# A two-layer decode kernel fed by one transfer queue: a new load order and new buffer places at the layer ends, and a longer rotation at the start of layer 2

## The chip, the cores and the metric

The kernel runs on one core of one Trainium2 chip. The metric is the device time of one execution in microseconds (us). Every run named here is fast, that is, not slowed by a lower granted clock.

The names of the profile are these. PE is TensorE (matrix multiply), PEld its weight loads, DVE is VectorE, ACT is ScalarE, and SP is SyncE, which here does nothing but issue transfers (DMA). "L356" is a line of the kernel that ran. The changed kernel has more lines, so the line that issues a whole K or V is L356 in the one and L359 in the other.

## The reference, cut to what matters

```python
# B, Sq, D = 2, 1, 576;  H, Sk, Dh = 32, 16384, 128;  F = 4608;  all bf16
def _A_ref(x, k_cache, v_cache, wq, wo):                    # attention over a cache
    q = (x @ wq).reshape(B, Sq, H, Dh).transpose(0, 2, 1, 3)
    scores = einsum("bhqd,bhkd->bhqk", q, k_cache) * (Dh ** -0.5)
    o = einsum("bhqk,bhkd->bhqd", softmax(scores), v_cache)
    return o.transpose(0, 2, 1, 3).reshape(B, Sq, H * Dh) @ wo
def _B_ref(x, w1, w2, w3, w4):                              # mixer and MLP
    ...                                                     # hs: small, from w2
    x1 = x + hs
    return x1 + gelu(layernorm(x1) @ w3) @ w4               # w3: 576 x 4608, w4: 4608 x 576

x = A_x                                                     # two layers, the same weights
x = x + _A_ref(layernorm(x), A_k_cache, A_v_cache, A_wq, A_wo)
x = x + _B_ref(layernorm(x), B_w1, B_w2, B_w3, B_w4)
x = x + _A_ref(layernorm(x), A_k_cache, A_v_cache, A_wq, A_wo)
x = x + _B_ref(layernorm(x), B_w1, B_w2, B_w3, B_w4)
```

Each pair of batch and head is a *unit*: 64 units a layer, each with a K of 4 MB and a V of 4 MB. The caches are read once per layer, and little is computed per byte.

## The kernel before

K(i) and V(i) stand below for the K and V of the unit at position i (0 to 63) of its layer. Layer 2 takes the units in reverse order and keeps the last two units of layer 1, so its own loads begin with K(2).

The on-chip buffer is three *places* (thirds). Each holds a K in its front half and a V in its back half. All loads go through one list in program order, on one queue:

```python
def pump(self):                              # the load list
    while self.queue:
        keys, p, n, src, sem = self.queue[0]
        under = [t for t in self.live if t["off"] < p + n and p < t["off"] + t["n"]]
        if not all(t["done"] for t in under):
            return                           # the head waits, and so does everything behind it
        ...                                  # issue it, after the last readers of what lies under it
```

This says where a unit goes, and what follows the last unit:

```python
def place(self, l, i):
    if l == 0:
        return 2 if i == self.U - 1 else i % 2
    return (2, 0, 1, 2, 0)[i] if i < 5 else (2, 1)[i % 2]
...
def want_w34(l, p):                          # w3, then w4 in pieces of 5, 4, 2, 1
    base = p * self.place_n
    rows("w3", l, self.w3, base)
    at, a0 = base + (2 * KT - 1) * self.F // 2, 0
    for c, n in enumerate(self.W4_PIECES):
        ...
        if c == 1:
            at = base                        # later pieces of w4 go over w3
...
for l in range(2):
    wp = 2 - 2 * l                           # the place of wo
    early = 5 if l == 1 else 0
    for i in range(U):
        kv("K", l, i, split=(l == 1 and i == 2))
        if i < early:
            kv("V", l, i)
        elif i - 1 >= early:
            kv("V", l, i - 1)
        ...                                  # pieces of wo; the last one where a V of place wp begins
    kv("V", l, U - 1)
    want_w34(l, 1 if l == 0 else 0)
    if l == 0:
        want_wq(1, 1)
```

In a unit, chunks 0 to 7 of K are transposed on PE, copied by ACT and multiplied on PE; chunks 8 to 15 are a multiply and a reduce each on DVE (a *pair*). The V of the unit before is weighed at the end of the unit:

```python
for i in range(U):
    ...
    dv = list(range(NCP, NCH))               # chunks 8 to 15, for DVE
    for c in range(NCP):                     # c = 0 to 7
        self.turn(l, i, c)                   # transpose chunk c
        ...
        if c >= 1:
            for _ in range(-(-len(dv) // (NCP - c))):
                self.dots(l, i, dv.pop(0))   # two pairs at c == 1, then one each
    if i >= 1:
        self.weigh(l, i - 1, 0)
    while self.waiting:
        self.score()
    if i >= 1:
        self.weigh(l, i - 1, 1)
    if i == U - 2:
        self.project_pieces(l, [self.n_wo - 1])   # last piece of wo
    ...
self.unit_max(l, U - 1)
self.exps(l, U - 1)
for h in range(2):
    self.weigh(l, U - 1, h)
self.project_last(l)
```

## Time and profile before

| before | value |
|---|---|
| time, median of 4 runs | 2590.79 us (2590.68 to 2591.45) |
| span of the profiled run | 2588.8 us |
| transfer queue busy | 99.1% of the span |
| bytes through it | 1097.76 MB |
| rate where nothing disturbs it (525 to 925 us) | 431 GB/s |
| those bytes at that rate | 1097.76 / 0.431 = 2547 us |
| DVE busy, PE busy | 76%, 59% |

These are lines of the profile's page: busy time of the engines with their instruction counts, bandwidth in 40 equal slices of the span, the main queue (packets, MB, share), and the chain of work that ended last. The last two are DVE's reduce and multiply among the costliest groups, with busy time and the mean of one in ns.

```profile
PE 1539.4 (59%) x34519; PEld 1451.9 (56%) x34519; DVE 1977.0 (76%) x2775; ACT 1111.4 (43%) x1809; POOL 0.8 (0%) x10
...
GB/s 415 429 427 432 431 431 430 429 434 431 431 430 431 430 431 432 430 432 401 423 395 359 433 432 430 431 430 431 433 430 432 430 432 430 430 433 432 429 424 343
...
q1 hardware_dynamic: 51224, 1097.76, 99.1%
...
DMA 54%; DVE 37%; PE 8%; issue 1%; ACT 0%; SPq 0%; DVEq 0%
...
L697 DVE TENSOR_REDUCE sd<-prod 128x8 f32<-128x1024 bf16 x1024 | 1249.1, 1220 | 35.5
...
L694 DVE TENSOR_TENSOR prod<-buf,qb 128x1024 bf16<-128x1024 bf16 x1024 | 697.5, 681 | 10.8 <-DMA buf<-in_A_k_cache_dram 9.9
```

The transfers are the limit: 2547 of 2588.8 us go by if the queue never pauses. A 4 MB load lands every 9.7 us, so the two loads of a unit take 19.4 us. Eight DVE pairs take 14.85 us (1.855 us a pair in the timeline, where the multiply and the reduce overlap a little). The Trainium skill's page "DMA: Bandwidth & Descriptors", section "Specifications", gives 435 GB/s as the ceiling of the fabric; the 431 GB/s of this trace lies just under it. So nothing but the dips in the bandwidth row is to be won: slice 21 (395, from 1294 us on, the layer change), slice 22 (359, from 1359 on, the start of layer 2) and the last. Slice 19 (401) dips too, but the loads around it land 9.7 us apart, so it costs nothing.

This is the windows view of before. Columns: the stretch and its length, busy us of PE, PEld, DVE, ACT and POOL (with instruction counts), granted clock of PE, share of the DMA engines, GB/s.

```profile
525.00:925.00 400.00, 231.69 (x5180) 219.38 (x5180) 307.34 (x421) 173.21 (x280) 0.00 (x0) 0.66 1.00 431
...
1268.00:1272.00 4.00, 2.31 (x46) 1.71 (x43) 3.93 (x5) 4.00 (x9) 0.00 (x0) 1.00 1.06 459
1272.00:1276.00 4.00, 3.18 (x120) 3.18 (x121) 3.90 (x6) 0.63 (x1) 0.00 (x0) 0.63 0.95 406
...
1296.00:1300.00 4.00, 3.15 (x114) 3.06 (x111) 0.23 (x1) 0.49 (x2) 0.00 (x0) 0.50 0.69 216
...
1405.00:1420.00 15.00, 9.76 (x241) 9.26 (x239) 13.84 (x19) 8.08 (x14) 0.00 (x0) 0.73 0.33 125
...
2570.00:2575.00 5.00, 3.65 (x125) 3.63 (x126) 0.88 (x7) 0.50 (x2) 0.00 (x0) 0.50 0.16 45
```

These are the issues of SP in the timeline of before, at the start of layer 2 (start, us, line, what, how many in a row):

```profile
1367.84 16.84 SPq L356 DMA_DIRECT2D buf<-in_A_k_cache_dram  x2
1384.72 0.43 SPq L356 DMA_DIRECT2D buf<-in_A_v_cache_dram  x1
1417.37 0.33 SPq L356 DMA_DIRECT2D buf<-in_A_k_cache_dram  x1
1417.74 0.43 SPq L356 DMA_DIRECT2D buf<-in_A_v_cache_dram  x1
```

The largest hole is here. K(6) and V(5) are issued by 1384.72 and land at 1400.6 and 1410.3. K(7) goes where unit 5 still computes, is issued at 1417.37 and lands at 1431.0, 20.7 us after V(5) where 9.7 is normal: 11 us lost. At 1296 to 1300 and at 2570 to 2575 the later pieces of w4 wait for w3, over which they go.

### The profile page before, as it was taken

Reading aid. Unit: us, or ns where it says so; the run is one execution under the profiler, and the core shown is the slowest. Engines: PE = TensorE matmul, PEld = TensorE weight load, DVE = VectorE, ACT = ScalarE, POOL = GpSimd, SP = SyncE. Lnnn points to the kernel's source line nnn. Section 1 sums busy time; section 2 is a strip of 40 time slices with the busy share of each in tenths; the row PEclk is TensorE's granted clock in tenths of the full one; section 3 lists DMA queues with packets and bytes.
Section 4 is the critical chain, followed back from the end, with each engine's and each line's share of the span. In section 5 each row is a group of like instructions: output and inputs, shape, how many; then the busy total and the mean of one; then the engine's idle time right before and its main releaser. Section 6 shows DMA issues by size and latency. Waiting matters only on the chain.

```text
span 2588.8 us, 75423 instructions
## 1 busy us (share of the span) xinstructions
PE 1539.4 (59%) x34519; PEld 1451.9 (56%) x34519; DVE 1977.0 (76%) x2775; ACT 1111.4 (43%) x1809; POOL 0.8 (0%) x10
## 2 busy tenths in 40 slices
PE   5656555655565556657567655556555655555575
PEld 4555555655555555546567555555554555555565
DVE  5877787778777777877759877877777777778775
ACT  4444443444444444444335444444443444444442
POOL 0000000000000000000000000000000000000000
PEclk8666666666666666666656666666666666666665
DMA  9999999999999999999998999999999999999998
GB/s 415 429 427 432 431 431 430 429 434 431 431 430 431 430 431 432 430 432 401 423 395 359 433 432 430 431 430 431 433 430 432 430 432 430 430 433 432 429 424 343
DMA packets 51322, 1099.05 MB, mean 425 GB/s; under 512 B 4820, under 2 KB 13080, under 8 KB 16792
## 3 DMA queue, kind: packets, MB, share of 16 engines
q1 hardware_dynamic: 51224, 1097.76, 99.1%
q8 instruction: 59, 0.97, 0.1%
q14 instruction: 39, 0.32, 0.0%
HBM read 1097.74 MB, written 0.00 MB: 424 GB/s over the span
## 4 chain that ended last, share of the span: by engine, by line
DMA 54%; DVE 37%; PE 8%; issue 1%; ACT 0%; SPq 0%; DVEq 0%
DMA buf<-in_A_k_cache_dram 50%; DVE sd L697 23%; DVE prod L694 13%; PE tps L665 4%; DMA buf<-in_A_v_cache_dram 2%; PE misc L715 2%; DVE small L717 1%; DMA buf<-in_A_wq_dram 1%; PE ops L738 1%; PE misc L575 0%; DMA buf<-in_B_w_dram 0%; PE sps L539 0%; SPq L370 0%; PE misc L505 0%; DVE small L709 0%
## 5 line engine op out<-in xcount | busy, mean ns | idle before, releaser
L669 ACT ACTIVATE ktsb<-tps 128x1024 bf16<-128x1024 bf16 x1024 | 1004.7, 1028 | 859.9 <-PE tps L665 854.0
L697 DVE TENSOR_REDUCE sd<-prod 128x8 f32<-128x1024 bf16 x1024 | 1249.1, 1220 | 35.5
L665 PE MATMUL tps<-ident,buf 128*128 128x128 bf16 x8192 | 833.2, 269 | 668.5 <-DMA buf<-in_A_k_cache_dram 665.8
L665 PEld LDWEIGHTS tps<-ident,buf 128*128 128x128 bf16 x8192 | 676.3, 123 | 698.2 <-DMA buf<-in_A_k_cache_dram 687.3
L694 DVE TENSOR_TENSOR prod<-buf,qb 128x1024 bf16<-128x1024 bf16 x1024 | 697.5, 681 | 10.8 <-DMA buf<-in_A_k_cache_dram 9.9
L738 PE MATMUL ops<-p,buf 128*128 128x1 bf16 x16384 | 467.5, 165 | 194.7 <-DMA buf<-in_A_v_cache_dram 180.4
L738 PEld LDWEIGHTS ops<-p,buf 128*128 128x128 bf16 x16384 | 448.7, 102 | 205.8 <-DMA buf<-in_A_v_cache_dram 188.7
L682 PE MATMUL sps<-qcur,ktsb 128*128 128x1 bf16 x8192 | 350.5, 166 | 91.3 <-ACT ktsb L669 83.1
L717 DVE TENSOR_REDUCE small<-misc 128x1 f32<-128x128 f32 x128 | 37.3, 292 | 478.8 <-PE misc L715 478.8
L682 PEld LDWEIGHTS sps<-qcur,ktsb 128*128 128x128 bf16 x8192 | 314.6, 102 | 130.2 <-ACT ktsb L669 128.3
L653 ACT ACTIVATE qb<-misc 128x128 bf16<-128x128 f32 x128 | 35.5, 278 | 519.8 <-PE misc L650 519.8
L715 PE MATMUL misc<-identS,small 128*128 128x128 f32 x256 | 95.6, 477 | 41.0 <-DVE small L709 41.0
L715 PEld LDWEIGHTS misc<-identS,small 128*128 128x128 f32 x256 | 69.7, 332 | 44.2 <-DVE small L709 35.5
L726 ACT ACTIVATE p<-sps,small 128x64 bf16<-128x64 f32 x128 | 40.7, 318 | 19.4 <-DVE small L717 19.4
L726 ACT ACTIVATE p<-sd,small 128x64 bf16<-128x64 f32 x128 | 45.3, 354 | 0.0
L645 ACT ACTIVATE qcur<-qt 128x1 bf16<-128x1 bf16 x128 | 29.1, 227 | 19.3 <-DVE qt L582 19.3
L650 PE MATMUL misc<-ident,qcur 128*128 128x128 bf16 x128 | 34.2, 267 | 1.6 <-ACT qcur L645 1.1
L705 DVE TENSOR_REDUCE small<-sps 128x1 f32<-128x64 f32 x128 | 27.4, 214 | 0.0
L726 ACT ACTIVATION_READ_ACCUMULATOR p<-sps,small 128x1 f32 x128 | 27.1, 211 | 0.0
L707 DVE TENSOR_REDUCE small<-sd 128x1 f32<-128x64 f32 x128 | 26.6, 208 | 0.0
L726 ACT ACTIVATION_READ_ACCUMULATOR p<-sd,small 128x1 f32 x128 | 26.4, 207 | 0.0
L745 DVE COPY o<-ops 128x1 f32<-128x1 f32 x128 | 18.9, 148 | 9.3 <-PE ops L738 9.3
(74 smaller groups left out, 158.8 us busy)
## 6 DMA issues: line engine op xcount, KB each, us to landing
buf<-in_A_v_cache_dram SPq DMA_DIRECT2D x126, 4096.0 KB, 31.9
buf<-in_A_k_cache_dram SPq DMA_DIRECT2D x125, 4096.0 KB, 22.5
buf<-in_B_w_dram SPq DMA_DIRECT2D x8, 1152.0 KB, 30.1
buf<-in_A_wq_dram SPq DMA_DIRECT2D x8, 1024.0 KB, 10.3
buf<-in_A_wo_dram SPq DMA_DIRECT2D x14, 576.0 KB, 32.8
buf<-in_B_w_dram SPq DMA_DIRECT2D x2, 2160.0 KB, 36.9
buf<-in_A_k_cache_dram SPq DMA_DIRECT2D x2, 2048.0 KB, 16.1
buf<-in_B_w_dram SPq DMA_DIRECT2D x2, 1728.0 KB, 8.1
```

The lines of the kernel that those rows point to most:

```text
L645: self.act(lambda a: a.activation(out=self.qcur[:, q:q + 1], in_=self.qt[:, u:u + 1], func=ACT.Copy), r=["qt"], w=[f"qcur{q}"])
L650: self.pe(lambda pe: pe.matmul(self.misc[:, 0:128], lhsT=bcast(self.qcur[:, q:q + 1], 128), rhs=self.ident[:, :], start=True, stop=True), ...
L653: self.act(lambda a: a.activation(out=self.qb[q][:, :], in_=self.misc[:, 0:128], func=ACT.Copy), r=["P:misc"], w=[f"qb{q}"])
L665: ins = pe.transpose(self.tps[b][:, j * 128:(j + 1) * 128], kt[:, (j0 + j) * 128:(j0 + j + 1) * 128], self.ident[:, :])
L669: self.act(lambda a: a.activation(out=self.ktsb[k][:, :, :].rearrange("p a b -> p (a b)"), in_=self.tps[b][:, :], func=ACT.Copy), r=[f"P:t ...
L682: ins = pe.matmul(self.sps[sp][:, col:col + 1], lhsT=self.ktsb[k][:, j, :], rhs=self.qcur[:, sp:sp + 1], start=True, stop=True)
L694: self.dve(lambda v: v.tensor_tensor(out=self.prod[d][:, :, :], in0=k3, in1=bcast_mid(self.qb[q][:, :], self.CH), op=ALU.mult), r=[*res, f ...
L697: self.dve(lambda v: v.tensor_reduce(out=self.sd[q][:, o:o + self.CH], in_=self.prod[d][:, :, :], axis=AX.X, op=ALU.add), r=[f"prod{d}"], ...
L715: self.pe(lambda pe: pe.matmul(self.misc[:, 128:256], lhsT=bcast(self.m[:, q:q + 1], 128), rhs=self.identS[:, :], start=True, stop=True), ...
L717: self.dve(lambda v: v.tensor_reduce(out=self.bias[:, q:q + 1], in_=self.misc[:, 128:256], axis=AX.X, op=ALU.max, negate=True), r=["P:misc ...
L726: self.act(lambda a, c0=c0, c1=c1, src=src, part=part: a.activation(out=self.p[q][:, c0:c1], in_=src, func=ACT.Exp, bias=self.bias[:, q:q ...
L738: ins = pe.matmul(self.ops[q][:, 0:1], lhsT=vt[:, j * 128:(j + 1) * 128], rhs=self.p[q][:, h * self.TB + j:h * self.TB + j + 1], start=(h ...
```

## The change

Its intent is to close these holes. It does five things.

1. Layer 2's first 12 units rotate over three places instead of mostly two.
2. In units 1 to 4 of layer 2, V is weighed earlier, so that its place is free sooner.
3. The later pieces of w4 go, in layer 2, into a free place instead of over w3 (and w3 itself into place 1 instead of 0).
4. At both layer ends the last K is loaded ahead of the last three Vs, and the last K and the last V come in halves. The last piece of wo, used at the end of the last unit but one in before, is now used within the last unit. The last V goes over this piece in both layers; in before it did so in layer 1 alone, and in layer 2 it changes place.
5. The wo pieces before it are used two units sooner, and the last normalizers are computed before the last V is weighed.

```diff
     def place(self, l, i):
+        if i == self.U - 1:
+            return 2 - 2 * l
         if l == 0:
-            return 2 if i == self.U - 1 else i % 2
-        return (2, 0, 1, 2, 0)[i] if i < 5 else (2, 1)[i % 2]
+            return i % 2
+        return (2, 0, 1)[i % 3] if i < self.ROT else (2, 1)[i % 2]      # ROT = 12
...
                 if c == 1:
-                    at = base
...
+                    at = p1 * self.place_n
...
-                kv("K", l, i, split=(l == 1 and i == 2))
+                kv("K", l, i, split=(l == 1 and i == 2) or i == U - 1)
                 if i < early:
-                    kv("V", l, i)
-                elif i - 1 >= early:
+                    kv("V", l, i, split=(l == 1 and i == 2))
+                elif early <= i - 1 < U - 3:
                     kv("V", l, i - 1)
...
-            kv("V", l, U - 1)
-            want_w34(l, 1 if l == 0 else 0)
+            for i in range(U - 3, U):
+                kv("V", l, i, split=i == U - 1)
+            want_w34(l, 1, 1 if l == 0 else 2)
...
+            early = l == 1 and 1 <= i <= 4
...
-                if i >= 1 and c == 4:
+                if i >= 1 and c == (3 if early else 4):
                     self.exps(l, i - 1)
...
+                if early and c == 5:
+                    self.weigh(l, i - 1, 0)
+                    self.weigh(l, i - 1, 1)
+                if i == U - 1 and c == 5:
+                    self.weigh(l, i - 2, 0)
+                    self.weigh(l, i - 2, 1)
+                    self.project_pieces(l, [self.n_wo - 1])
...                                          # wo from unit 13 on in layer 2; normalizers() and normalize() split from project()
```

More of the change, by code (lines that the diff above doesn't have):

```diff
@@ L239 @@
     N_MID = 3
+    ROT = 12
     WO_PIECE = 4
@@ L373, in want_wq, with want_w34 @@
             rows("wq", l, self.wq, p * self.place_n + unit, last=p * self.place_n + 7 * unit // 8)
-        def want_w34(l, p):
+        def want_w34(l, p, p1):
             base = p * self.place_n
@@ L381, in want_w34 @@
                 if c == 1:
-                    at = base
-                assert at + m <= (p + 1) * self.place_n
+                    assert at <= base + self.place_n
+                    at = p1 * self.place_n
                 ap = self.w4[a0 * 128 * self.FJ:(a0 + n) * 128 * self.FJ, :].rearrange(
@@ L405, in plan @@
             early = 5 if l == 1 else 0
-            gap = max(1, (U - 16) // self.n_wo)
+            wo_at = 7 if l == 0 else self.ROT + 1
+            gap = max(1, (U - 8 - wo_at) // self.n_wo)
             for i in range(U):
-                kv("K", l, i, split=(l == 1 and i == 2))
+                kv("K", l, i, split=(l == 1 and i == 2) or i == U - 1)
                 if i < early:
-                    kv("V", l, i)
-                elif i - 1 >= early:
+                    kv("V", l, i, split=(l == 1 and i == 2))
+                elif early <= i - 1 < U - 3:
                     kv("V", l, i - 1)
-                j, r = divmod(i - 7, gap)
+                j, r = divmod(i - wo_at, gap)
                 if r == 0 and 0 <= j < self.n_wo:
@@ L743, in weigh, with normalizers @@
         self.release("V", l, u, h)
-        if h == 1:
+        if h == 1 and i < self.U - 1:
             self.dve(lambda v: v.tensor_copy(out=self.o[:, u:u + 1], in_=self.ops[q][:, 0:1]),
                      r=[f"P:ops{q}"], w=["o"])
-    def project(self, l, h0, h1, parts):
-        B, D, KT = self.B, self.D, self.KT
-        u0, u1 = h0 * B, h1 * B
+    def normalizers(self, u0, u1):
         dps = self.misc[:, 320:320 + 2 * (u1 - u0)]
@@ L760, in project, with normalize @@
         self.dve(lambda v: v.reciprocal(out=den, in_=den), r=["den"], w=["den"])
-        self.dve(lambda v: v.tensor_tensor(out=self.otn[:, u0:u1], in0=self.o[:, u0:u1], in1=den, op=ALU.mult),
-                 r=["den", "o"], w=["otn"])
+    def normalize(self, u0, u1, o, res):
+        self.dve(lambda v: v.tensor_tensor(out=self.otn[:, u0:u1], in0=o, in1=self.den[:, u0:u1], op=ALU.mult),
+                 r=["den", res], w=["otn"])
+    def project(self, h0, h1, parts):
+        B, D, KT = self.B, self.D, self.KT
         out = self.misc[:, 256:256 + KT * B]
@@ L783, in project_pieces @@
         parts.sort(key=lambda p: p[0])
-        self.project(l, parts[0][0], parts[-1][0] + parts[-1][1], parts)
-    def project_last(self, l):
-        h = self.order[l][-1] // self.B
-        self.project(l, h, h + 1, [(h, 1, self.wolast[:, :], ["wolast"], lambda: None)])
+        h0, h1 = parts[0][0], parts[-1][0] + parts[-1][1]
+        u0, u1 = h0 * self.B, h1 * self.B
+        self.normalizers(u0, u1)
+        self.normalize(u0, u1, self.o[:, u0:u1], "o")
+        self.project(h0, h1, parts)
     def attention(self, l):
@@ L794, in attention @@
         self.query_rows(l, 0)
-        first, last = 2 + 4 * l, U - 6
+        first, last = (2, self.ROT)[l], U - 8
+        assert first < last and (last - first) % 2 == 0
         self.s.loops.append((l * U + first, (last - first) // 2, 2))
@@ L818, in attention @@
                         self.dots(l, i, dv.pop(0))
-            if i >= 1:
+                if early and c == 5:
[5 more added lines that the diff above has]
+                    self.project_pieces(l, [self.n_wo - 1])
+            now = i >= 1 and not early and i != U - 2
+            if now:
                 self.weigh(l, i - 1, 0)
@@ L822, in attention @@
                 self.score()
-            if i >= 1:
+            if now:
                 self.weigh(l, i - 1, 1)
-            if i == U - 2:
-                self.project_pieces(l, [self.n_wo - 1])
             if i + 1 < U:
@@ L830, in attention @@
         self.s.tag = None
+        u, h = self.order[l][-1], self.order[l][-1] // self.B
         self.unit_max(l, U - 1)
         self.exps(l, U - 1)
-        for h in range(2):
-            self.weigh(l, U - 1, h)
-        self.project_last(l)
+        self.normalizers(h * self.B, (h + 1) * self.B)
+        other = self.order[l][-2]
+        self.normalize(other, other + 1, self.o[:, other:other + 1], "o")
+        self.weigh(l, U - 1, 0)
+        self.weigh(l, U - 1, 1)
+        q = (U - 1) % 2
+        self.normalize(u, u + 1, self.ops[q][:, 0:1], f"P:ops{q}")
+        self.project(h, h + 1, [(h, 1, self.wolast[:, :], ["wolast"], lambda: None)])
 def bass_interleave_layers__mha_block_cached__mixer_s_mlp__decode_kernel(
```

## The prediction

> **What bounds it now.** The transfer queue: the page's queue part shows it busy for 99.1% of the span; 1097.8 MB at the undisturbed 431 GB/s (windows 525 to 925 us) are 2547 us of 2588.8. A 4 MB K or V lands every 9.7 us; a unit's compute is about 16.5 us (eight DVE multiply and reduce pairs, 0.68 and 1.22 us) against 19.45 us for its two loads. Only holes in the landings can be won. From the queue's timeline and landing times:
> - Start of layer 2, the largest: K and V issued at 1384.4 and 1384.7 land at 1400.6 and 1410.3; the next K is issued only at 1417.37 (its third is still read by the unit two before) and lands at 1431.0: 11.0 us lost. Loads 1334 to 1352 lose 3.5 more.
> - Between layers w4's later pieces wait for w3: about 1 us.
> - End: last V lands at 2558.5, w4's later pieces are issued at 2573.75, DMA share is 0.16 in 2570 to 2575; the end is 30.3 us after that V.
> - The dip at 1204 to 1208 costs nothing: landings around it (1203.9, 1213.6, 1223.2) keep pace.
>
> **What the change does.** Bytes and arithmetic stay.
> - Layer 2's first 12 units rotate over three thirds: the late K waits for unit 4 (read by 1401), not 5 (1417): minus 11 us. Earlier weighing in units 1 to 4: minus 1.
> - w4's later pieces in layer 2 find a free third: w3 and w4 (10.6 MB, 25 us) follow the last V unbroken, with 4 us after the last piece: 29 us; the compute chain, 2.4 us shorter by half V and early normalizers, fits below. Tail: minus 1.5. Between layers: minus 1.
> - A new wait. The last V goes over the last wo piece in both layers, now used in the last unit, behind V(61). On DVE its normalization stands behind six of eight dot pairs. Worked out: last but one K lands, +2.65 us DVE start, +14.85 eight pairs, +2.0 unit change, +11.1 six pairs, +1.5 normalization and projection = 32.1 us. K63, V61, V62 have landed after 29.2. So the half V is issued 3 us after the queue ran dry; issue to landing on a dry queue costs 3.9 us over the pure transfer (13.6 against 9.7 at 1417). Loss: 6.9 us per layer, nearly 14. The Trainium skill, "DMA: Bandwidth & Descriptors", section "Anatomy of one DMA", says the issuing sequencer waits on semaphores, not the DMA engines, so w3 and w4 wait behind it; the trace agrees (w4's issue at 1296.68 holds back wq's, 1299.69).
>
> **Sum.** 11 + 1 + 1 + 1.5 gained, about 1 from smaller holes, 14 lost: minus 2 us. The new wait may be smaller, so I lean lower: **2587 us, 2577 to 2593**. Faster by over 2%: 0.01; within: 0.98; slower: 0.01.
>
> **What would show it.** Right: no empty queue at 1405 to 1420. The last V's first half issued right after the second small projection, after V(62) landed, with some 6 us of idle DMA at about 1272 to 1278 and 2543 to 2549; layer 2's unit 0 starting 5 us later than 1320.5; no idle DMA in 2570 to 2575. Wrong: the half V issued before V(62) lands; the time would be near 2575.
>
> **What would make it wrong.** The projection reached earlier; longer PE instruction stalls in the longer unrolled parts (1 to 3 us each, "issue"), delaying it; a compute-bound tail.

## The result and the profile after

| | before | after |
|---|---|---|
| median of 4 runs, us | 2590.79 (2590.68 to 2591.45) | 2588.56 (2587.28 to 2589.91) |
| ratio, with 95% interval | | 0.9991 (0.9974 to 1.0008) |
| span of the profiled run, us | 2588.8 | 2588.1 |

A ratio here is the mean time of one kernel's fast runs over that of the other's of the same rounds, so it is not quite the ratio of the medians quoted. The medians differ by 2.2 us, within 2%; the interval includes 1, so the times alone do not show that the change is faster at all. The four runs of after lie in two groups (2589.91 and 2589.72; 2587.28 and 2587.41), which none of the experiments explains; the profile is of a run of the upper group, and the median lies between the two. A difference to it is therefore good to some 1.2 us.

These are the lines of after's page for bandwidth, queue and chain:

```profile
GB/s 412 431 429 431 430 431 430 431 433 431 431 430 430 431 431 433 430 428 409 371 420 428 429 425 434 431 429 431 432 432 429 430 434 431 431 430 433 418 427 324
...
q1 hardware_dynamic: 51944, 1097.76, 99.1%
...
DMA 52%; DVE 40%; PE 6%; SPq 1%; issue 1%; ACT 0%; DVEq 0%
```

The dip of slice 22 (359) is gone, and slice 21 is up from 395 to 420. In exchange slice 20 has fallen from 423 to 371, and the last slice from 343 to 324. "SPq" is now 1% of the chain, but that is no sign of the hole: 0.8% is at L390, the issues of w4, which hold SP long (see the last section), and experiment 3 shows the same 1% without the hole. The busy share of the queue, 99.1% in both, shows nothing of all this. These are windows of after (columns as above):

```profile
1264.00:1268.00 4.00, 4.00 (x109) 4.00 (x108) 3.93 (x6) 3.40 (x7) 0.00 (x0) 0.50 0.80 344
1268.00:1272.00 4.00, 1.96 (x59) 1.86 (x56) 3.93 (x5) 0.00 (x0) 0.00 (x0) 0.50 0.11 45
1272.00:1276.00 4.00, 2.07 (x37) 2.08 (x38) 3.21 (x9) 0.60 (x1) 0.00 (x0) 0.50 0.32 61
1276.00:1280.00 4.00, 4.00 (x145) 4.00 (x143) 2.36 (x3) 1.45 (x2) 0.00 (x0) 0.50 0.85 340
...
1296.00:1300.00 4.00, 3.26 (x115) 3.24 (x116) 0.41 (x3) 0.38 (x2) 0.00 (x0) 0.50 1.01 415
...
1405.00:1420.00 15.00, 13.36 (x272) 12.83 (x270) 13.83 (x19) 9.18 (x16) 0.00 (x0) 0.61 1.02 436
...
2570.00:2575.00 5.00, 2.08 (x73) 1.93 (x70) 1.26 (x4) 0.49 (x2) 0.00 (x0) 0.50 1.02 414
```

The three holes of before are closed: 436 instead of 125 GB/s at 1405 to 1420, 415 instead of 216 at 1296 to 1300, 414 instead of 45 at 2570 to 2575. A new one has opened at 1264 to 1280, where before moved 386 to 459 GB/s in every 4 us. After's four windows moved (344 + 45 + 61 + 340) x 4 = 3160 KB, where 431 GB/s would have moved 6896 KB: 8.7 us of transfer are missing. Layer 2 has the same hole: at 2536 to 2548 the three windows show 160, 10 and 135 GB/s.

This is the timeline of after at the end of layer 1, cut to what leads to the issue of the last V:

```profile
1272.08 1.22 DVE L702 TENSOR_REDUCE sd<-prod 128x8 f32<-128x1024 bf16 x1
1273.22 0.15 DVE L750 COPY o<-ops 128x1 f32<-128x1 f32 x1
1273.28 0.16 DVE L760 TENSOR_REDUCE den<-misc 128x6 f32<-128x12 f32 x1
1273.48 0.19 DVE L762 RECIPROCAL den<-den 128x6 f32<-128x6 f32 x1
1273.70 0.17 DVE L765 TENSOR_TENSOR otn<-o,den 128x6 bf16<-128x6 f32 x1
...
1273.93 0.56 PE L580 MATMUL misc<-otn,buf 128*128 128x2 bf16 x15 [3.96 <-DVE otn L765]
...
1274.52 1.56 SPq L356 DMA_DIRECT2D buf<-in_A_v_cache_dram  x2
```

Before had the same projection a unit earlier, at 1260.91, and its last V left at 1261.50, 21 us before it was to land:

```profile
1260.91 0.56 PE L575 MATMUL misc<-otn,buf 128*128 128x2 bf16 x15 [3.02 <-DVE otn L761]
...
1261.50 0.33 SPq L356 DMA_DIRECT2D buf<-in_A_v_cache_dram  x1
```

In after the projection (15 matmuls, 0.56 us) reads the last piece of wo. Its operand is normalized on DVE in program order, behind six of the last unit's eight pairs. The last V may not land on the piece before the projection has read it. So a 2 MB half V, and behind it the other half, the 14 weight loads of w3, w4 and wq, and layer 2's first loads wait for a small DVE operation. The first half lands at 1282.3, 9.2 us after V(62), where 4.9 us is normal; the second at 1288.1.

These are the issues of SP at the start of layer 2, and the last V of layer 2, in after:

```profile
1389.92 0.33 SPq L359 DMA_DIRECT2D buf<-in_A_k_cache_dram  x1
1390.30 0.42 SPq L359 DMA_DIRECT2D buf<-in_A_v_cache_dram  x1
1406.44 0.33 SPq L359 DMA_DIRECT2D buf<-in_A_k_cache_dram  x1
...
2544.93 0.80 SPq L356 DMA_DIRECT2D buf<-in_A_v_cache_dram  x2
```

K(7) is now issued at 1406.44, before V(5) has landed (1414.3), and lands at 1425.2: a step of 10.9 us instead of 20.7. Layer 2's first matmul starts at 1326.13 instead of 1320.62, though: layer 1's end has taken 5.5 us.

### The profile page after: what moved, and what is told of

Same layout as the page of the kernel before. It is cut to its first block, busy times and chain, and to the rows that moved or that the text cites. A ratio compares the mean times of both kernels' runs of the same rounds, so it can differ in the third digit from the quotient of the medians.

```text
span 2588.1 us, 75341 instructions
## 1 busy us (share of the span) xinstructions
PE 1549.2 (60%) x34519; PEld 1463.6 (57%) x34519; DVE 1977.2 (76%) x2775; ACT 1112.9 (43%) x1809; POOL 0.8 (0%) x10
## 3 DMA queue, kind: packets, MB, share of 16 engines
q1 hardware_dynamic: 51944, 1097.76, 99.1%
## 4 chain that ended last, share of the span: by engine, by line
DMA 52%; DVE 40%; PE 6%; SPq 1%; issue 1%; ACT 0%; DVEq 0%
DMA buf<-in_A_k_cache_dram 49%; DVE sd L702 25%; DVE prod L699 14%; PE tps L670 4%; PE misc L720 2%; DMA buf<-in_B_w_dram 2%; DVE small L722 1%; SPq L390 1%; DMA buf<-in_A_wq_dram 1%; PE misc L580 0%; SPq L373 0%; DVE small L714 0%; DVE small L712 0%; SPq L356 0%; DVE small L710 0%
## 5 line engine op out<-in xcount | busy, mean ns | idle before, releaser
L670 PE MATMUL tps<-ident,buf 128*128 128x128 bf16 x8192 | 846.1, 271 | 647.4 <-DMA buf<-in_A_k_cache_dram 639.6
L670 PEld LDWEIGHTS tps<-ident,buf 128*128 128x128 bf16 x8192 | 686.0, 124 | 678.6 <-DMA buf<-in_A_k_cache_dram 662.5
L544 PE MATMUL sps<-xn,buf 128*128 128x2 bf16 x544 | 16.4, 166 | 14.0 <-DMA buf<-in_A_wq_dram 9.5
```

What stands on the lines that cost most here:

```text
L670: ins = pe.transpose(self.tps[b][:, j * 128:(j + 1) * 128], kt[:, (j0 + j) * 128:(j0 + j + 1) * 128], self.ident[:, :])
```

## The experiments

**The theory** is the prediction's: the rotation wins some 11 us, and the new wait for the last piece of wo loses nearly all of it, at two places.

**The rivals.** (a) The rotation is worth much less, as another limit takes over at once. (b) The loss comes from the new order itself (K ahead, halves, more transfers) and not from the wait. (c) The tail is bound by w3 and w4 or by compute, so that an earlier last V wins nothing.

Before was run again with each batch, with medians of 2591.16 (first batch), 2590.92 (second) and 2591.33 (third). Each batch ran on another chip. After itself was timed in its own batch, against 2590.79; differences to it, and between kernels of different batches, are of medians across batches. The 95% intervals are all against before and some 4 us wide either way. A difference under that between two changed kernels (experiments 7 to 9) rests on the narrow spread of their runs, 0.3 to 1.0 us within a kernel, and on the landings in the traces. (Only after, with 2.6 us, and experiment 6, with 1.8, spread more.) The outputs are right.

### 1. Rotation undone (first batch)

```diff
-        return (2, 0, 1)[i % 3] if i < self.ROT else (2, 1)[i % 2]
+        return (2, 0, 1)[i % 3] if i < 5 else (2, 1)[i % 2]
```

> The changed kernel with the rotation of layer 2's places stopped after unit 4, as the kernel before had it. Theory (the rotation removes an 11 us hole in the transfers at the start of layer 2, and all of it reaches the end because the transfer queue bounds the kernel): about 2600 us, 11 us over the changed kernel's 2588.6, with one load of a K issued near 1422 us instead of 1406. Rival (time won there is absorbed later, since buffers fill up and the queue waits for compute anyway): about 2589 us.

Measured: 2600.70 us (2600.39 to 2601.09), ratio to before 1.0037 (1.0020 to 1.0054). That is 12.1 us over after by the medians, and 11.0 between the two profiled runs (2600.89 and 2589.91). This is the issue of K(7) in its timeline:

```profile
1423.09 0.33 SPq L359 DMA_DIRECT2D buf<-in_A_k_cache_dram  x1
```

The late issue is back (1423.09 against 1406.44). The rotation holds what the rest loses; without it the change is slower than before.

### 2. The rotation alone (first batch)

```diff
# from the kernel before
-        return (2, 0, 1, 2, 0)[i] if i < 5 else (2, 1)[i % 2]
+        return (2, 0, 1)[i % 3] if i < 12 else (2, 1)[i % 2]
...
-                j, r = divmod(i - 7, gap)
+                j, r = divmod(i - (7 if l == 0 else 13), gap)
...
-        first, last = 2 + 4 * l, U - 6
+        first, last = (2, 12)[l], U - 6
```

> The kernel before with the rotation alone. Theory: about 2579 us (2590.8 minus 11 to 11.5), faster than the whole change, since nothing of the new wait at the layer ends is in it. Rival (the rotation gains little, and the change's small gain comes from the layer ends): 2588 to 2591 us.

Measured: 2582.78 us (2582.55 to 2582.93), ratio 0.9967 (0.9951 to 0.9984). It wins 8.4 us, where 11 to 11.5 was expected: a miss. The last V landed only 9.6 us earlier (2548.84 against 2558.47), and the end came 32.1 us after it (span 2580.9) instead of 30.4. PE's timeline just after the last V landed:

```profile
2548.97 3.05 PE L738 MATMUL ops<-p,buf 128*128 128x1 bf16 x109 [1.57 <-DMA buf<-in_A_v_cache_dram]
2555.10 0.65 PE L738 MATMUL ops<-p,buf 128*128 128x1 bf16 x19 [3.08 <-issue]
```

Amid 128 matmuls whose data were there, PE stood still for 3.08 us ("issue": it waited for nothing that the profile shows). Before has such a stall too, of 2.27 us and just behind the 128 matmuls; the projection that follows starts 8.0 us after the last V's landing here and 6.4 in before. All that follows is a chain: w3's matmuls came later, and with them the later pieces of w4, which go over w3; the first of them landed 6.5 us after w4's first piece (5.7 in before). So 1.7 us of what the rotation wins were lost in a tail bound by compute. Experiment 9 tests this.

### 3. The last V kept apart from the last piece of wo (first batch)

The piece moves to the end of the V area, so that the first half V finds nothing under it and only the second waits.

```diff
-   want_wo(l, j, wp * self.place_n + (unit if j == self.n_wo - 1 else j * self.WO_PIECE * D))
+   want_wo(l, j, wp * self.place_n + (2 * unit - self.N_MID * D if j == self.n_wo - 1 else j * self.WO_PIECE * D))
```

> The changed kernel with the last wo piece at the end of the V area, so that only the second half of the last V waits for the last small projection. Theory (the hole ahead of the last V costs 6.4 us per layer and all of it is in the bounding queue): about 2576 us, 12 to 13 us under the changed kernel; first half issued near 1238, second near 1275 before the first half has landed. Rival one (the last unit's exponentials are ready only at 1282.9, so compute bounds the layer end and only about 3.3 us per layer come back): about 2582 us. Rival two (the hole comes from the order of loads, not from where the wo piece lies): about 2589 us.

Measured: 2578.22 us (2577.75 to 2578.46), ratio 0.9950 (0.9933 to 0.9966): 10.3 us under after. SP's timeline at the end of layer 1 has the first half V early, at 1239.58; the second was held until the projection, and left at 1274.40 within this group:

```profile
1239.58 35.15 SPq L356 DMA_DIRECT2D buf<-in_A_v_cache_dram  x2
```

The second half landed at 1282.7, against 1288.1 in after. Nothing else was edited, so the wait is the cause of the loss. The time is 2 us over the theory's 2576, and nearer to it than to the 2582 of rival one.

### 4. The K order of before kept (first batch)

The last K is no longer loaded ahead, and the last piece of wo is used at the end of the last unit but one, as in before. The halves, the early normalizers and all else stay.

```diff
-                elif early <= i - 1 < U - 3:
+                elif early <= i - 1:
...
-            for i in range(U - 3, U):
-                kv("V", l, i, split=i == U - 1)
+            kv("V", l, U - 1, split=True)
...
-                if i == U - 1 and c == 5:
-                    self.weigh(l, i - 2, 0)
-                    self.weigh(l, i - 2, 1)
-                    self.project_pieces(l, [self.n_wo - 1])
-            now = i >= 1 and not early and i != U - 2
+            now = i >= 1 and not early
...
+            if i == U - 2:
+                self.project_pieces(l, [self.n_wo - 1])
```

> The changed kernel with the last K in its old order, the last projection piece back at the end of the last but one unit, and nothing else undone. Theory: the new wait is gone although the last V still goes over the last wo piece (issued near 1262, some 10 us before the V ahead of it lands), so about 2576 us, as with the moved wo piece. Rival (the K ahead is worth time by itself, because the last unit starts earlier): 2580 us or more.

Measured: 2577.61 us (2577.38 to 2577.79), ratio 0.9948 (0.9931 to 0.9965). The last V's halves were issued at 1261.46, and landed at 1277.7 and 1282.6. Without the K ahead the kernel is 11 us faster than after (the theory had 2576). Its windows at the two critical stretches:

```profile
1268.00:1272.00 4.00, 1.60 (x38) 1.34 (x34) 3.93 (x6) 3.63 (x8) 0.00 (x0) 0.86 1.01 422
...
1292.00:1296.00 4.00, 3.43 (x117) 3.40 (x118) 0.41 (x3) 0.21 (x2) 0.00 (x0) 0.50 0.81 326
```

There is no hole before the last V, and a shallow one later, where w4 waits for w3. That one costs nothing: w4's second piece landed 4.2 us after the first, as in an unbroken stream.

### 5 and 6. The projection placed earlier and later (second batch)

The cleanest test of the wait changes nothing but its length: one character moves the last piece's projection in DVE's program order. At c == 2 it stands behind three pairs, at 5 behind six, at 7 behind eight.

```diff
-                if i == U - 1 and c == 5:
+                if i == U - 1 and c == 2:       # experiment 5
+                if i == U - 1 and c == 7:       # experiment 6
```

> The changed kernel with the weighing of V61 and the last small projection three chunks earlier in the last unit, behind three dot pairs of DVE instead of six. The wo piece stays under the last V. Theory (the time of the projection on DVE sets when the last V is issued): issue near 1269 and not 1274.5, some 4 us before V62 lands, hole gone, 2578 to 2580 us. Rival (the overlap of places itself keeps the queue dry): 2588 us.

> The opposite dose: the last small projection two chunks later, behind all eight dot pairs. Theory: the last V is issued two pairs, 3.7 us, later in each layer (near 1278.2), and the whole of it reaches the end: 2588.6 plus 7.4 is 2596 us. Rival (the last unit's exponentials, ready at 1282.9, bound the layer end, so the V has slack): 2589 to 2591 us.

Measured: with c == 2, 2577.55 us (2577.34 to 2577.67), ratio 0.9949 (0.9932 to 0.9965), level with experiment 4 as the fastest. With c == 7, 2595.84 us (2594.92 to 2596.73), ratio 1.0020 (1.0003 to 1.0036). The issue of the last V of layer 1 with c == 2:

```profile
1268.77 1.05 SPq L356 DMA_DIRECT2D buf<-in_A_v_cache_dram  x2
```

and with c == 7:

```profile
1277.97 0.80 SPq L356 DMA_DIRECT2D buf<-in_A_v_cache_dram  x2
```

| projection at | pairs before it | last V issued (layer 1) | its second half lands | time, us |
|---|---|---|---|---|
| c == 2 | 3 | 1268.77 | 1282.7 | 2577.55 |
| c == 5 (after) | 6 | 1274.52 | 1288.1 | 2588.56 |
| c == 7 | 8 | 1277.97 | 1291.7 | 2595.84 |

Three pairs are 3 x 1.855 = 5.6 us: the issue moved by 5.75 us, the landing by 5.4 and the time, with two layer ends, by 11.0. Two pairs are 3.7 us: 3.45, 3.6 and 7.3. In this range a microsecond of wait costs a microsecond at each layer end.

These are windows with c == 2:

```profile
1268.00:1272.00 4.00, 3.82 (x66) 3.82 (x67) 3.28 (x6) 2.31 (x5) 0.00 (x0) 0.50 0.63 188
1272.00:1276.00 4.00, 4.00 (x130) 3.83 (x129) 3.93 (x5) 3.11 (x6) 0.00 (x0) 0.93 1.02 426
...
1296.00:1300.00 4.00, 0.70 (x26) 0.61 (x23) 1.26 (x4) 0.49 (x2) 0.00 (x0) 0.50 1.02 413
```

A smaller dip is left at 1268 to 1272 (188 GB/s); from 1264 to 1280 some (6896 - (344 + 188 + 426 + 426) x 4) / 431 = 3.2 us of transfer are missing. The gap at w4 is gone (413 against 216 in before). Yet the dip costs nothing: V(62) and the halves land at 1272.9, 1277.8 and 1282.7, in steps of 4.9 us as in an unbroken stream. In the trace's packet records V(62) ends with 16 packets of 4 bytes, from 1266.6 to 1272.4, and its landing is recorded 0.5 us after the last of them. The core has 16 DMA engines, so this reads as one such packet from each, the engines being done up to 5.8 us apart. On this reading bandwidth falls once the engines that are ahead run dry, and a landing is late only if the last of them runs dry too. Experiment 5 gains nothing over experiment 4 because the landings keep pace in both. Layer 2's first matmul starts at 1320.44 here, at 1320.27 in experiment 4 and at 1320.62 in before.

### 7. w4 over w3 again, wait shortened (second batch)

```diff
# from experiment 3
-            want_w34(l, 1, 1 if l == 0 else 2)
+            want_w34(l, 1, 1)
```

> The version with the moved wo piece (2578.2 us), with w4's later pieces over w3 in layer 2 too, as the kernel before had it. Theory (with the half V and the early normalizers w3 is used up some 4 us before w4's first piece has landed, so the free third is hardly needed any more): 2578 to 2579 us. Rival (the free third is what closed the hole in the tail): 2580 us or more, with w4's second piece landing 5.5 us or more after the first instead of 4.2.

Measured: 2577.93 us (2577.88 to 2578.14), ratio 0.9950 (0.9934 to 0.9967), 0.3 us under experiment 3. The second piece was issued at 2559.65 and landed 4.2 us after the first, no later than it must. With the chain of compute shortened by the half V and the early normalizers, w3 is read in time, and the free place for w4 is worth nothing. Without them it is worth 3.1 us (experiment 9).

### 8. Early weighing of V undone, wait shortened (second batch)

```diff
# from experiment 3
-            early = l == 1 and 1 <= i <= 4
+            early = False
```

> The version with the moved wo piece (2578.2 us), without the earlier weighing in layer 2's units 1 to 4. Theory: V of the fourth unit is issued some 2.5 us later (1347.6 instead of 1345.1) and lands 1 to 2 us later, and this reaches the end: 2579 to 2580 us. Rival (a tie: the K behind it is late anyway): 2578.2 us.

Measured: 2580.70 us (2580.45 to 2580.93), ratio 0.9961 (0.9944 to 0.9977): 2.5 us over experiment 3. The issue of V(3) in this run is

```profile
1349.00 0.33 SPq L359 DMA_DIRECT2D buf<-in_A_v_cache_dram  x1
```

and in experiment 3 it is

```profile
1345.10 0.33 SPq L359 DMA_DIRECT2D buf<-in_A_v_cache_dram  x1
```

V(3) and K(4) then land in steps of 11.5 and 11.3 us, against 10.4 and 9.7 in experiment 3. So K(4) lands some 2.4 us later than there (1372.3 against 1369.9), and the end of the trace is 2.4 us later too. The theory had 1 to 2 us.

### 9. The rotation with the free place for w4 (third batch, 5 rounds)

```diff
# from experiment 2
-        def want_w34(l, p):
+        def want_w34(l, p, p1):
...
-                    at = base
-                assert at + m <= (p + 1) * self.place_n
+                    at = p1 * self.place_n
...
-            want_w34(l, 1 if l == 0 else 0)
+            want_w34(l, 1 if l == 0 else 0, 1 if l == 0 else 2)
```

> The kernel before with the rotation (2582.8 us) and, added, w4's later pieces in a free third in layer 2. The rotation alone moved the landing of the last V by 9.7 us but the end by 7.9 us only; the trace shows a PE stall of 3.1 us inside the last weighing, after which w4's second piece, waiting for w3, landed 6.5 us after the first. Theory (the stall reaches the end because that piece waits on PE): with the free third the pieces land 4.2 us apart, compute then bounds the tail, and about 1.5 us come back: 2581 us. Rival (the free third is worth nothing, as in the version with the moved wo piece): 2582.8 us.

Measured: 2579.69 us (2579.50 to 2580.49), ratio 0.9956 (0.9943 to 0.9970): 3.1 us under experiment 2, where the theory had 1.5 and the rival none. The PE stall is still there (2.81 us). What has gone is the wait for w4: its second piece lands 4.1 us after the first, and PE's timeline shows its matmuls in one run,

```profile
2569.63 4.96 PE L574 MATMUL misc<-prod,buf 128*128 128x2 bf16 x180 [2.01 <-DVE prod L604]
```

180 matmuls in 4.96 us. The end comes 29.2 us after the last V, against 32.1 in experiment 2 and 30.4 in before. So the tail's part of experiment 2's miss came from w4, which had to wait for w3 in a chain of compute. Undoing that gives back 1.7 us; the rest of the 3.1 us is mostly a tail shorter than before's. The other part of the miss, a last V that landed 9.6 us earlier and not 11, is not explained by it. Rotation and free place together win 11.6 us (2591.33 - 2579.69).

### What became of the rivals

Rival (a), a rotation worth much less, falls with experiment 1 (12.1 us). Rival (b), a loss from the new order itself, falls with experiments 3, 5 and 6: with the order kept and only the wait changed, the time moves over 18 us, and experiment 4 shows the old order no faster than the new one with a short wait. Rival (c), a tail bound by compute, holds for a part: with before's tail it took 1.7 us of the rotation's gain, and the free place for w4 is worth 3.1 us there (experiments 2 and 9); with the new tail it takes nothing (experiment 7).

## Why the prediction was right

The sum came out: 2587 us was predicted, with 2577 to 2593, and 2588.56 was measured. The mechanism that the prediction named, a gain of the rotation and a new wait at both layer ends, is shown by experiments 1, 3, 5 and 6. Several terms were mis-sized, and the errors partly cancel; that the sum came so near is partly luck.

| term, us | predicted | measured | from |
|---|---|---|---|
| rotation | -11 | -9.8 at the landing of K(7); -12.1 undone in after; -8.4 alone; -11.6 with w4's free place | traces; exp. 1, 2, 9 |
| early weighing | -1 | -2.5 | exp. 8 |
| smaller holes | about -1 | not measured apart | |
| between layers (last V to the end of wq) | -1 | -0.1: from 36.8 to 36.6 | traces |
| tail (last V to the end) | -1.5 | -0.9: from 30.4 to 29.5 | traces |
| new wait, each of two ends | +6.9 | +5.4 to 5.5 | exp. 3, 5 |
| sum | -2 (stated lower: 2587, or -3.8) | -2.2 | |

The measured terms come from different kernels and need not add up to -2.2. One account does add up: how far after's landings lie behind before's in the two traces. It is +5.5 us at the last piece of wq in layer 1, +4.0 at V(5), -5.8 at K(7), -5.2 at V(62) of layer 2, +0.2 at the last V and -0.7 at the end. So in these two runs the new wait cost 5.5 and 5.4 us, the rotation gave 9.8, the start of layer 2 ahead of it 1.5, and the tail 0.9; some 0.5 was lost between K(7) and V(62).

- **What bounds the kernel.** The transfers, as said: the time moved where the landings moved, but for some 1.7 us in the tail (experiment 2).
- **The chain to the new wait** was right. From the landing of the last K but one, 32.1 us were worked out; the trace has 1274.52 - 1242.9 = 31.6.
- **The step "So the half V is issued 3 us after the queue ran dry; issue to landing on a dry queue costs 3.9 us over the pure transfer"** was mis-sized, both ways. The recorded landing of V(62) was 1273.0 instead of the 1272.1 that the prediction's 29.2 us gave, so the issue came 1.5 us after it, not 3. The 3.9 us was read from a 4 MB load; the 2 MB half took 7.7 us from issue to landing, 2.8 over the 4.9 of the stream. The second half lost another 1.0 (5.9 against 4.9). The sum, 1.5 + 2.8 + 1.0 = 5.3, stands in place of 6.9.
- **"some 6 us of idle DMA at about 1272 to 1278"** took the recorded landing for the end of the bytes. The bandwidth had fallen to 45 GB/s at 1268 to 1272, some 5 us ahead of that landing, and V(62)'s 16 packets of 4 bytes lie from 1266.8 to 1272.6. So 8.7 us of transfer are missing. Of these, 3.2 are missing with c == 2 as well, where the landings keep pace. The other 5.5 are what the landings and the time show.
- **Head of line.** The prediction drew on the Trainium skill's page "DMA: Bandwidth & Descriptors", section "Anatomy of one DMA": the wait sits in the issuing sequencer, not in the DMA engines. The trace agrees: w3, w4 and wq all left after the half V (w3's first at 1276.12, when the 1.56 us of the half Vs' issue were over).
- **"layer 2's unit 0 starting 5 us later than 1320.5"**: it started at 1326.13, 5.5 us later.
- **"Wrong: the half V issued before V(62) lands; the time would be near 2575"** was tested from the other side: with the issue early (experiments 3 to 5) the time is 2577.6 to 2578.2.
- **What the rest of the layer ends' rework is worth.** Experiment 9 has none of it and none of the early weighing: 2579.69. Less the 2.5 us of the early weighing it would be at 2577.2 (an estimate from experiments 8 and 9); the best kernel with the rework is at 2577.55. By this estimate K ahead, half V and early normalizers together won about nothing here, even without their wait; no run tests it directly.

A version beats both kernels: after with its projection at c == 2 (2577.55 us), or with the old order of the last K (2577.61). Both are 13.4 to 13.6 us under before.

**What stays open.** In the kernels with the rotation one step near K(7) or V(6) is still 10.9 to 11.2 us instead of 9.7; it was not traced to a cause. It is why K(7) gained 9.8 us and not 11. The two groups of after's times are unexplained. Nor is the cause of PE's stalls shown. It was not tried whether c == 1 or a projection outside the last unit would do still better.

## What to carry to other kernels

When a kernel is bound by one in-order queue, ask of each load not how soon it is wanted but what lies under it and when the last reader of that runs; a 0.56 us projection behind six DVE pairs cost 5.5 us at each of two layer ends and gave back nearly all that a better rotation had won. Then look where that reader stands in its engine's program order: here moving it by three places was worth 11 us, for one character. The busy share of the queue (99.1% before and after) hides such holes; bandwidth in windows of a few us, and the issue times of the queue's timeline, show them. What a hole costs is read from the landings: with c == 2 a dip of 3.2 us cost nothing.

## What the Trainium skill lacked or had wrong

- "DMA: Bandwidth & Descriptors", section "Anatomy of one DMA", gives a fit of 2.0 us plus bytes / 436e3 for one DMA, for transfers that GpSimd issues, and none for the SP queue used here. The fit gives 6.8 us for 2 MB and 11.6 for 4 MB. Here a load on a queue run dry took 7.7 us for 2 MB (layer 1's last V in after) and 13.6 for 4 MB (before's K(7)), against 4.9 and 9.7 in an unbroken stream.
- The same page, section "Where 436 GB/s comes from", says that the HBM side, about 358 GB/s, binds for transfers from HBM, though the same paragraph quotes a measured 425. This kernel read from HBM at 431 GB/s over 400 us, with one core at work. The page "HBM Reference", section "Specifications (TRN2)", does say that a core alone goes above its share, with about 425 GB/s; the trace agrees with that page.
- The same page, section "Why a DMA increments its semaphore by 16 and not by 1", says that the 16 engines of a DMA finish independently, and gives no size for the spread. Here the 16 packets of 4 bytes at the end of V(62), a 4 MB load, lie from 1266.8 to 1272.6 in after's trace, a spread of 5.8 us; the landing was recorded at 1273.0, while the bandwidth was at 45 GB/s from 1268 on.
- "Runtime: NRT & Kernel Launch", section "Instruction fetch mechanics", calls the cost of crossing an instruction block mostly hidden. PE stood still for 3.08 us amid 128 unrolled matmuls whose operands were there (experiment 2), and for 2.81 us in experiment 9. That fetching is the cause is not shown; no page gives a stall of that size.
- No page gives a figure for how long an issue can hold SP (it would belong to "Perfetto Trace Analysis", section "DMA Instruction — HWDGE (DVE, Sync)"). In after's layer 2, the second piece of w4 held it for 11.43 us, on an instruction that waits for no semaphore; its landing was in time (4.2 us after the first piece).
